# A different instruction order for a chunked attention and wave-MLP kernel on one core

## Chip, cores, metric

One core of one Trainium2 chip. The metric is device time in microseconds (us) of one execution. Times quoted as "profile" times count from the start of the profiled execution's span; the span is some 1.8 us shorter than the timed execution.

## The reference

q, k and v have the shape 8 x 8 heads x 576 x 64. Attention runs within chunks of 64 rows; its output x (8 x 576 x 512) goes through a phase mixing:

```
scores = (q_c @ k_c.T) / 8                  # in chunks of 64 rows
attn   = softmax(scores);  x = attn @ v_c   # x: 8 x 576 x 512
theta  = x @ w_theta                        # 512 x 512
y      = w_tok_r @ (x * cos(theta)) + w_tok_i @ (x * sin(theta))   # 576 x 576
u      = x + y
out    = u + max(u @ w_ch, 0)               # 512 x 512
```

## The kernel before

The work is cut into 327 items. A string, ORDER, lists them; the kernel emits them in that order, so each engine has its own share of the items in that order. Two batches make a pair p (0 to 3), and a pair's rows are cut into five groups g, taken as two 128-row tiles, or one for the middle group, g = 2. An item reads `kind.p.g:bits`:

- `lq`, `lv`: load q and k, or v, of a group; `lw`, `lc`, `lt`: load w_theta, w_ch, w_tok. POOL issues these.
- `a1`: transpose q and k on PE into PSUM, copy both halves out. `a2`: scores on PE, exp on ACT. `a3.p.g.h`: attention times v on PE, reciprocal and product on DVE, giving x.
- `a4`: transpose x (on PE and copied, or by DMA). `a5`: theta on PE, cos and sin on ACT. `z`: x times cos or sin on DVE.
- `tw`: transpose w_tok on PE. `yh` (a half of the columns, only for the first batch) and `y`: the token matmuls and the sum with x. `w`, `ut`, `st`: u @ w_ch, u transposed by DMA, the rest and the store.

The bits say which engine copies: for `a1`, bit 1 puts q's copy on ACT (else DVE), bit 2 puts k's on DVE (else ACT), bit 32 cuts the transposes to 64 x 64 pieces. The parts that the argument touches (cuts marked with `# ...`):

```python
psum = ctx.enter_context(tc.tile_pool(name="psum", bufs=4, space=bass.MemoryType.PSUM))

def psum2(name, dtype=FP32):          # four buffers of 4 KB per partition, in turn
    n = 1024 if dtype == FP32 else 2048
    return psum.tile([P, n], dtype, name=name, tag="ps")

def load_w(ap, f16):
    nc.gpsimd.dma_start(f16, ap.rearrange("(a p) e -> p a e", p=P))

def copy(eng, out, in_):
    if eng: nc.vector.tensor_copy(out=out, in_=in_)
    else:   nc.scalar.copy(out=out, in_=in_)

def a1(p, g, bits):
    ps = psum2("ps_qkT", FP16)
    # ... transposes of q (w = 0) and k (w = 1)
    copy(not bits & 1, qT[...], psv[:, 0, :, :, 0:n])
    copy(bits & 2,     kT[...], psv[:, 1, :, :, 0:n])

def a5(p, g):
    ps = psum2("ps_theta")
    # ... 4 matmuls of 512 columns per 128-row tile, 8 for a group of two tiles
    nc.scalar.activation(out=cos, in_=pin, func=AF.Sin, bias=pihalf, scale=1.0)
    nc.scalar.activation(out=sin, in_=pin, func=AF.Sin)

for n, item in enumerate(ORDER):
    name, bits = item.split(":")
    kind, *args = name.split(".")
    # ...
    emit[kind](*args)
```

The softmax here doesn't subtract the row's maximum and nothing guards it: scores larger than these inputs give would overflow.

Of the kernel before, what the change touches and what calls it, by code (L numbers as in the profile page):

```python
# [16 lines left out]


ORDER = """
lq.0.0:0 lq.0.2:0 lq.0.1:0 a1.0.0:35 lv.0.2:0 lv.0.0:0 lv.0.1:0 lw.0:0 a1.0.2:1 lq.0.3:0  # L20
a2.0.0:0 a2.0.2:0 lq.0.4:0 lt.0.1:0 a1.0.1:2 a3.0.2.0:0 a2.0.1:0 a3.0.0.0:0 a3.0.0.1:0
a3.0.1.0:0 a4.0.2:0 tw.0.0:1 a3.0.1.1:0 lt.1.1:0 lv.0.4:0 a4.0.0:33 a5.0.2:0 a4.0.1:33
z.0.2.0:0 lv.0.3:0 a5.0.0:0 a1.0.3:2 z.0.0.0:0 a5.0.1:0 a1.0.4:3 z.0.1.0:0 z.0.1.1:0
tw.0.2:0 tw.0.1:1 lt.1.0:0 a2.0.4:0 z.0.0.1:0 tw.1.1:0 a2.0.3:0 yh.0.0:0 a3.0.4.0:0
a3.0.4.1:0 yh.0.1:0 tw.1.2:0 a4.0.4:1 a3.0.3.0:0 a3.0.3.1:0 tw.1.0:1 a5.0.4:0 a4.0.3:1
yh.1.0:0 lq.1.0:0 z.0.4.0:0 a1.1.0:0 lq.1.2:0 lq.1.1:0 a1.1.2:1 lq.1.3:0 lc.0:0
z.0.4.1:0 a5.0.3:0 a1.1.1:2 lv.1.2:0 a2.1.0:0 yh.1.1:0 z.0.3.0:0 lv.1.0:0 z.0.3.1:0
a2.1.1:0 lq.1.4:0 a1.1.3:3 lv.1.1:0 lv.1.3:0 a2.1.2:0 lq.2.0:0 w.0.0:0 st.0.0:0
y.0.1.0:0 a3.1.2.0:0 a3.1.0.0:0 lq.2.2:0 lv.1.4:0 lv.2.1:0 w.0.1:0 st.0.1:0 a3.1.0.1:0
w.0.2:0 lq.2.1:0 st.0.2:0 y.0.1.1:0 a4.1.2:32 lv.2.2:0 a3.1.1.0:0 a1.1.4:0 a3.1.1.1:0  # L30
w.0.3:0 st.0.3:0 y.0.1.2:0 lq.2.3:0 a2.1.4:0 a2.1.3:0 a4.1.0:1 a4.1.1:1 a5.1.2:0
a3.1.3.0:0 a1.2.0:2 lv.3.1:0 a5.1.1:0 a3.1.4.0:0 a3.1.4.1:0 lv.2.0:0 y.0.1.3:0 a4.1.4:33
a1.2.2:1 a3.1.3.1:0 w.0.4:0 a5.1.0:0 st.0.4:0 lv.2.3:0 z.1.2.0:0 a1.2.1:3 a4.1.3:33
lq.2.4:0 w.0.5:0 a5.1.4:0 z.1.0.0:0 z.1.1.0:0 z.1.0.1:0 w.0.6:0 st.0.5:0 z.1.1.1:0
st.0.6:2 a5.1.3:0 z.1.3.0:0 lq.3.0:0 y.1.0.0:0 lv.3.4:0 a2.2.2:0 a1.2.3:32 a2.2.1:0
z.1.3.1:0 z.1.4.0:0 z.1.4.1:0 lq.3.2:0 y.1.0.1:0 lv.3.3:0 lq.3.1:0 w.0.7:0 a2.2.0:0
st.0.7:0 a2.2.3:0 y.1.1.0:0 a3.2.2.0:0 a3.2.1.0:0 y.1.1.1:0 a3.2.0.0:0 a3.2.1.1:0
y.1.0.2:0 a4.2.2:0 a3.2.0.1:0 lq.3.3:0 lv.3.2:0 a1.2.4:32 w.0.8:0 st.0.8:0 a5.2.2:0
y.1.0.3:0 a4.2.0:1 a4.2.1:0 a1.3.0:0 a3.2.3.0:0 a1.3.2:1 w.1.0:0 a5.2.0:0 z.2.2.0:0
a5.2.1:0 st.1.0:0 z.2.1.0:0 a3.2.3.1:0 a2.2.4:0 lv.3.0:0 y.1.1.2:0 z.2.0.0:0 lv.2.4:0  # L40
z.2.0.1:0 w.1.1:0 st.1.1:0 y.1.1.3:0 z.2.1.1:0 a2.3.2:0 a2.3.0:0 a1.3.1:35 a3.3.2.0:0
w.1.2:0 lq.3.4:0 st.1.2:0 y.2.0.0:0 a3.3.0.0:0 a3.2.4.0:0 ut.1.1.3:0 y.2.0.1:0 a2.3.1:0
ut.1.1.2:0 a1.3.3:32 a4.2.3:17 a3.2.4.1:0 a4.2.4:16 y.2.0.2:0 a3.3.1.0:0 a2.3.3:0
a1.3.4:35 y.2.0.3:0 ut.1.1.1:0 a2.3.4:0 a3.3.0.1:0 w.1.3:0 st.1.3:2 a3.3.1.1:0
ut.1.1.0:0 w.1.4:0 a4.3.0:49 st.1.4:2 a5.2.3:0 a4.3.1:17 w.1.5:0 a5.2.4:0 a5.3.0:0
st.1.5:2 z.2.4.0:0 z.2.4.1:0 w.1.6:0 a5.3.1:0 w.1.7:0 ut.2.0.1:0 ut.2.0.0:0 z.2.3.0:0
z.2.3.1:0 st.1.6:2 ut.2.0.3:0 st.1.7:2 y.2.1.0:0 a3.3.3.0:0 ut.2.0.2:0 a3.3.4.0:0
y.2.1.1:0 a3.3.4.1:0 a4.3.2:16 a3.3.3.1:0 y.2.1.2:0 a5.3.2:0 w.1.8:0 a4.3.4:16 z.3.0.0:0
z.3.1.0:0 a4.3.3:16 z.3.2.0:0 st.1.8:0 ut.2.1.1:0 z.3.0.1:0 y.2.1.3:0 z.3.1.1:0 w.2.0:0
st.2.0:0 ut.2.1.2:0 a5.3.4:0 w.2.1:0 z.3.4.0:0 z.3.4.1:0 a5.3.3:0 ut.2.1.3:0 st.2.1:0  # L50
w.2.2:0 y.3.0.0:0 st.2.2:2 z.3.3.0:0 z.3.3.1:0 w.2.3:0 ut.2.1.0:0 y.3.0.1:0 w.2.4:0
st.2.3:0 y.3.0.2:0 w.2.5:0 ut.3.0.1:0 st.2.4:0 st.2.5:2 y.3.1.0:0 w.2.6:0 y.3.0.3:0
ut.3.0.2:0 st.2.6:2 ut.3.0.0:0 w.2.7:0 st.2.7:2 y.3.1.1:0 w.2.8:0 st.2.8:2 y.3.1.2:0
ut.3.0.3:0 ut.3.1.1:0 y.3.1.3:0 ut.3.1.0:0 w.3.0:0 st.3.0:2 w.3.1:0 w.3.2:0 ut.3.1.2:0
st.3.1:2 w.3.3:0 ut.3.1.3:0 st.3.2:0 w.3.4:0 st.3.3:0 st.3.4:0 w.3.5:0 w.3.6:0 st.3.5:2
st.3.6:2 w.3.7:0 w.3.8:0 st.3.7:0 st.3.8:0
""".split()


# [572 lines left out]
```

## Time and profile before

| | kernel before |
|---|---|
| timed runs | 209.69, 210.24, 213.06 us |
| profiled execution | 210.18 us, span 208.3 us, mean granted clock 0.971 |
| PE busy | 186.0 us of the span |

The busy table, the slices, the stretches and the waits are in the prediction below. These are lines of PE's timeline; the columns are start, length, engine, source line, operation, output and inputs, sizes, number of instructions, and in brackets the idle time before them and what ended it.

```profile
12.62 1.92 PE L295 MATMUL ps_qkT<-id,qk 128*64 128x128 f16 x32
...
21.83 1.89 PE L443 MATMUL ps_theta<-wtheta,xTm 128*128 128x512 f16 x4 [0.58 <-DMA wtheta<-in_moe_w_theta_dram]
24.38 2.37 PE L443 MATMUL ps_theta<-wtheta,xT 128*128 128x512 f16 x8
...
33.95 0.45 PE L325 MATMUL ps_sT<-qT,kT 64*64 64x64 f16 x32 [2.67 <-DVE kT L212]
...
35.47 1.79 PE L500 MATMUL ps_y<-wT,z 128*128 128x256 f16 x8
...
37.27 1.91 PE L500 MATMUL ps_y<-wT,z 128*128 128x256 f16 x8
...
58.96 2.12 PE L521 MATMUL ps_y<-wT,z 128*128 128x288 f16 x16
...
195.89 7.93 PE L552 MATMUL ps_uw<-wch,uT 128*128 128x512 f16 x36
```

The 32 transposes at 12.62 are item a1.0.1, the two theta groups a5.0.2 and a5.0.0, the 32 small matmuls at 33.95 item a2.0.4, and L500 is yh.0.0, the first real token matmul. Four theta matmuls take as long as eight should (1.89 us): the clock is halved there. yh.0.0's eight (and the eight of its second half at 37.27) take 1.79 and 1.91 us for the same reason, 1.5 us after the wait of 2.67 us. The line at 58.96 is item y.0.1.0, the one at 195.89 PE's last group.

### The profile page before, as it was taken

How to read it: one execution, taken by the hardware profiler on the slowest of the kernel's cores; microseconds unless marked ns; L12 is line 12 of the kernel's file. 1: busy time of each engine (PE TensorE's matmuls, PEld its weight loads, DVE VectorE, ACT ScalarE, POOL GpSimd, SP SyncE). 2: the span in 40 equal slices, each digit the busy share in tenths (PEclk: the TensorE clock that was granted, in tenths of full speed). 3: DMA queues.
4: the chain of work that ended last, by engine and by line, in shares of the span. 5: the costliest groups of instructions: out<-in, count | busy, mean ns of one | idle time of the engine just before them, and what ended most of it. 6: DMA issues, size and time to landing. Idle time of an engine off the chain costs nothing.

```text
span 208.3 us, 7055 instructions
## 1 busy us (share of the span) xinstructions
PE 186.0 (89%) x3150; PEld 124.4 (60%) x3150; DVE 131.2 (63%) x227; ACT 102.3 (49%) x110; POOL 93.5 (45%) x133
## 2 busy tenths in 40 slices
PE   0376894999999999999998999998999999999991
...
PEclk9997599799999999999999999999999999999998
...
GB/s 151 154 159 154 170 200 149 176 184 177 168 147 208 191 198 131 181 27 148 194 138 164 157 146 54 71 81 105 191 166 156 72 142 192 127 130 151 145 264 221
DMA packets 102141, 31.96 MB, mean 153 GB/s; under 512 B 95776, under 2 KB 98208, under 8 KB 102112
## 3 DMA queue, kind: packets, MB, share of 16 engines
...
HBM read 33.06 MB, written 9.44 MB: 204 GB/s over the span
## 4 chain that ended last, share of the span: by engine, by line
PE 70%; ACT 10%; DMA 6%; DVE 5%; issue 4%; POOL 3%; ACTq 0%; POOLq 0%
PE ps_y L521 27%; PE ps_uw L552 14%; PE ps_theta L443 13%; PE ps_y L500 4%; DMA wtheta<-in_moe_w_theta_dram 3%; PE ps_qkT L295 3%; DMA qk<-in_k_dram 3%; PE ps_x L354 3%; DVE kT L212 3%; POOL qk L169 2%; ACT eT L333 2%; PE ps_sT L325 2%; ACT qT L214 2%; ACT cos L453 2%; ACT sin L457 2%
## 5 line engine op out<-in xcount | busy, mean ns | idle before, releaser
L521 PE MATMUL ps_y<-wT,z 128*128 128x288 f16 x448 | 59.6, 286 | 0.3 <-DVE o L575 0.3
L521 PEld LDWEIGHTS <-z 128*128 128x128 f16 x448 | 42.8, 98 | 13.6 <-issue 0.3
L190 POOL DMA_DIRECT2D v<-in_v_dram x56 | 41.8, 773 | 16.1 <-DMA qk<-in_q_dram 6.8
...
L552 PE MATMUL ps_uw<-wch,uT 128*128 128x512 f16 x144 | 37.9, 380 | 0.1
L529 DVE TENSOR_TENSOR uT<-ps_y,xT 128x576 f16<-128x576 f32 x28 | 21.1, 755 | 19.0 <-PE ps_y L521 18.6
L443 PE MATMUL ps_theta<-wtheta,xT 128*128 128x512 f16 x128 | 30.6, 384 | 0.0
L453 ACT ACTIVATE cos<-ps_theta,pihalf 128x1024 f16<-128x1024 f32 (+1 forms) x20 | 20.6, 1031 | 19.6 <-PE ps_theta L443 18.1
L333 ACT ACTIVATE eT<-ps_sT 128x1024 f16<-128x1024 f32 (+1 forms) x20 | 23.1, 1197 | 13.0 <-PE ps_sT L325 12.9
L295 PE MATMUL ps_qkT<-id,qk 64*64 64x64 f16 (+1 forms) x832 | 20.1, 213 | 9.6 <-DMA qk<-in_q_dram 6.8
L368 DVE TENSOR_TENSOR x<-ps_x,recip 128x512 f16<-128x512 f32 x36 | 24.9, 691 | 1.2
L295 PEld LDWEIGHTS <-qk 64*64 64x64 f16 (+1 forms) x832 | 17.3, 114 | 12.4 <-DMA qk<-in_q_dram 6.5
L552 PEld LDWEIGHTS <-uT 128*128 128x128 f16 x144 | 14.0, 98 | 14.4
L212 DVE COPY kT<-ps_qkT 128x1024 f16<-128x1024 f16 x10 | 13.0, 1295 | 13.7 <-ACT qT L214 13.7
L169 POOL DMA_DIRECT2D qk<-in_q_dram x24 | 19.8, 830 | 2.5 <-PE ps_x L354 1.1
L443 PEld LDWEIGHTS <-xT 128*128 128x128 f16 x128 | 11.9, 99 | 14.5 <-DMA xT<-x 0.8
L169 POOL DMA_DIRECT2D qk<-in_k_dram x24 | 19.2, 805 | 1.2 <-issue 0.6
L457 ACT ACTIVATE sin<-ps_theta 128x1024 f16<-128x1024 f32 (+1 forms) x20 | 18.7, 936 | 0.0
L577 DVE SCALAR_TENSOR_TENSOR o<-ps_uw,un 128x512 f32<-128x512 f32 x23 | 15.7, 688 | 2.7 <-PE ps_uw L552 2.2
L468 DVE TENSOR_TENSOR z<-x,cos 128x1024 f16<-128x1024 f16 x16 | 10.8, 686 | 6.1 <-ACT cos L453 6.0
L214 ACT COPY kT<-ps_qkT 128x1024 f16<-128x1024 f16 (+1 forms) x10 | 10.8, 1084 | 6.3 <-DVE qT L212 6.3
L325 PE MATMUL ps_sT<-qT,kT 64*64 64x64 f16 x576 | 8.0, 198 | 5.9 <-DVE kT L212 5.6
...
## 6 DMA issues: line engine op xcount, KB each, us to landing
...
```

Of the source, the lines that this page charges most:

```text
L169: nc.gpsimd.dma_start(t[(pp // 2) : (pp // 2) + m // 2, ti].rearrange("p h t d -> p h (t d)"), src.rearrange("h (p t) d -> p h (t d)", t=2),)
L190: nc.gpsimd.dma_start(v16[pp : pp + m, sl, :, 0:D], v[2 * p + bb, :, s0 : s0 + m, :].rearrange("h s d -> s h d"),)
L212: nc.vector.tensor_copy(out=out, in_=in_)
L295: nc.tensor.transpose(psv[par * D : par * D + D, w, e, tk, r0 // CH : (r0 + step) // CH, :], t[rs, w, 2 * e + par, tk, :], id16[rs, rs],)
L333: nc.scalar.activation(out=eT.rearrange("p (r b s t) -> p r b t s", r=2, s=CH // 2, t=2), in_=ps.rearrange("p r (b t s) -> p r b t s", s=C ...
L368: nc.vector.tensor_tensor(out=xo, in0=px[:, :, :, 0:D], in1=recip.broadcast_to((P, 2, NE, D)), op=ALU.mult,)
L443: nc.tensor.matmul(ps[:, jj * DM : jj * DM + DM], xt[:, db, :], wtheta16[:, db, :], start=(db == 0), stop=(db == NDB - 1),)
L453: nc.scalar.activation(out=cos[:, 0:n].rearrange("p a e -> p (a e)"), in_=pin, func=AF.Sin, bias=pihalf, scale=1.0,)
L457: nc.scalar.activation(out=sin[:, 0:n].rearrange("p a e -> p (a e)"), in_=pin, func=AF.Sin)
L521: nc.tensor.matmul(psv[:, hf, 0:HS], zt[:, db * P : db * P + P], wT[:, kt, hf * HS : hf * HS + HS], start=(kt == 0), stop=(kt == 2 * KT),)
L529: nc.vector.tensor_tensor(out=uT_tile(p)[:, db, sl].rearrange("p (f c) -> p f c", f=2), in0=psv[:, :, 0:HS], in1=xT_tile(p)[:, db, sl].rea ...
L552: nc.tensor.matmul(ps[:, 0:DM], uT[:, db, j * P : j * P + P], wch16[:, db, :], start=(db == 0), stop=(db == NDB - 1),)
```

## The change

The intent: an order found by a search over a model with measured copy and exp times, that issues the first loads later, and that also has to do well in a second scenario where loads and copies take longer. Only the string changes; both strings hold the same 327 items, with other copy bits here and there. The start of the diff (the rest, all of the other items, is replaced in the same way and cut here):

```diff
 ORDER = """
-lq.0.0:0 lq.0.2:0 lq.0.1:0 a1.0.0:35 lv.0.2:0 lv.0.0:0 lv.0.1:0 lw.0:0 a1.0.2:1 lq.0.3:0
-a2.0.0:0 a2.0.2:0 lq.0.4:0 lt.0.1:0 a1.0.1:2 a3.0.2.0:0 a2.0.1:0 a3.0.0.0:0 a3.0.0.1:0
-a3.0.1.0:0 a4.0.2:0 tw.0.0:1 a3.0.1.1:0 lt.1.1:0 lv.0.4:0 a4.0.0:33 a5.0.2:0 a4.0.1:33
-z.0.2.0:0 lv.0.3:0 a5.0.0:0 a1.0.3:2 z.0.0.0:0 a5.0.1:0 a1.0.4:3 z.0.1.0:0 z.0.1.1:0
-tw.0.2:0 tw.0.1:1 lt.1.0:0 a2.0.4:0 z.0.0.1:0 tw.1.1:0 a2.0.3:0 yh.0.0:0 a3.0.4.0:0
+lq.0.0:0 lq.0.2:0 a1.0.0:35 a1.0.2:3 lq.0.1:0 a2.0.0:0 lv.0.2:0 a2.0.2:0 lv.0.0:0
+a1.0.1:1 a3.0.2.0:0 a3.0.0.0:0 lw.0:0 lv.0.1:0 a3.0.0.1:0 a4.0.2:1 lq.0.3:0 a2.0.1:0
+a4.0.0:33 a5.0.2:0 a3.0.1.0:0 a3.0.1.1:0 z.0.2.0:0 a5.0.0:0 lt.0.1:0 a4.0.1:33 a1.0.3:3
+z.0.0.0:0 tw.0.0:1 lq.0.4:0 lt.1.0:0 tw.0.2:1 a5.0.1:0 lv.0.3:0 lt.1.1:0 z.0.0.1:0
+lv.0.4:0 lq.1.0:0 z.0.1.0:0 z.0.1.1:0 lq.1.2:0 tw.0.1:1 a1.0.4:2 lq.1.1:0 a2.0.3:0
+lv.1.2:0 tw.1.0:0 yh.0.0:0 a2.0.4:0 a3.0.3.0:0 lc.0:0 lv.1.0:0 a3.0.3.1:0 lq.1.3:0
 ... (the other lines of both orders cut)
```

More of the change, by code (lines that the diff above doesn't have):

```diff
@@ L19 @@
 ORDER = """
-lq.0.0:0 lq.0.2:0 lq.0.1:0 a1.0.0:35 lv.0.2:0 lv.0.0:0 lv.0.1:0 lw.0:0 a1.0.2:1 lq.0.3:0
-a2.0.0:0 a2.0.2:0 lq.0.4:0 lt.0.1:0 a1.0.1:2 a3.0.2.0:0 a2.0.1:0 a3.0.0.0:0 a3.0.0.1:0
-a3.0.1.0:0 a4.0.2:0 tw.0.0:1 a3.0.1.1:0 lt.1.1:0 lv.0.4:0 a4.0.0:33 a5.0.2:0 a4.0.1:33
-z.0.2.0:0 lv.0.3:0 a5.0.0:0 a1.0.3:2 z.0.0.0:0 a5.0.1:0 a1.0.4:3 z.0.1.0:0 z.0.1.1:0
-tw.0.2:0 tw.0.1:1 lt.1.0:0 a2.0.4:0 z.0.0.1:0 tw.1.1:0 a2.0.3:0 yh.0.0:0 a3.0.4.0:0
-a3.0.4.1:0 yh.0.1:0 tw.1.2:0 a4.0.4:1 a3.0.3.0:0 a3.0.3.1:0 tw.1.0:1 a5.0.4:0 a4.0.3:1
@@ L26 @@
-yh.1.0:0 lq.1.0:0 z.0.4.0:0 a1.1.0:0 lq.1.2:0 lq.1.1:0 a1.1.2:1 lq.1.3:0 lc.0:0
-z.0.4.1:0 a5.0.3:0 a1.1.1:2 lv.1.2:0 a2.1.0:0 yh.1.1:0 z.0.3.0:0 lv.1.0:0 z.0.3.1:0
-a2.1.1:0 lq.1.4:0 a1.1.3:3 lv.1.1:0 lv.1.3:0 a2.1.2:0 lq.2.0:0 w.0.0:0 st.0.0:0
-y.0.1.0:0 a3.1.2.0:0 a3.1.0.0:0 lq.2.2:0 lv.1.4:0 lv.2.1:0 w.0.1:0 st.0.1:0 a3.1.0.1:0
-w.0.2:0 lq.2.1:0 st.0.2:0 y.0.1.1:0 a4.1.2:32 lv.2.2:0 a3.1.1.0:0 a1.1.4:0 a3.1.1.1:0
-w.0.3:0 st.0.3:0 y.0.1.2:0 lq.2.3:0 a2.1.4:0 a2.1.3:0 a4.1.0:1 a4.1.1:1 a5.1.2:0
@@ L32 @@
-a3.1.3.0:0 a1.2.0:2 lv.3.1:0 a5.1.1:0 a3.1.4.0:0 a3.1.4.1:0 lv.2.0:0 y.0.1.3:0 a4.1.4:33
-a1.2.2:1 a3.1.3.1:0 w.0.4:0 a5.1.0:0 st.0.4:0 lv.2.3:0 z.1.2.0:0 a1.2.1:3 a4.1.3:33
-lq.2.4:0 w.0.5:0 a5.1.4:0 z.1.0.0:0 z.1.1.0:0 z.1.0.1:0 w.0.6:0 st.0.5:0 z.1.1.1:0
-st.0.6:2 a5.1.3:0 z.1.3.0:0 lq.3.0:0 y.1.0.0:0 lv.3.4:0 a2.2.2:0 a1.2.3:32 a2.2.1:0
-z.1.3.1:0 z.1.4.0:0 z.1.4.1:0 lq.3.2:0 y.1.0.1:0 lv.3.3:0 lq.3.1:0 w.0.7:0 a2.2.0:0
-st.0.7:0 a2.2.3:0 y.1.1.0:0 a3.2.2.0:0 a3.2.1.0:0 y.1.1.1:0 a3.2.0.0:0 a3.2.1.1:0
@@ L38 @@
-y.1.0.2:0 a4.2.2:0 a3.2.0.1:0 lq.3.3:0 lv.3.2:0 a1.2.4:32 w.0.8:0 st.0.8:0 a5.2.2:0
-y.1.0.3:0 a4.2.0:1 a4.2.1:0 a1.3.0:0 a3.2.3.0:0 a1.3.2:1 w.1.0:0 a5.2.0:0 z.2.2.0:0
-a5.2.1:0 st.1.0:0 z.2.1.0:0 a3.2.3.1:0 a2.2.4:0 lv.3.0:0 y.1.1.2:0 z.2.0.0:0 lv.2.4:0
-z.2.0.1:0 w.1.1:0 st.1.1:0 y.1.1.3:0 z.2.1.1:0 a2.3.2:0 a2.3.0:0 a1.3.1:35 a3.3.2.0:0
-w.1.2:0 lq.3.4:0 st.1.2:0 y.2.0.0:0 a3.3.0.0:0 a3.2.4.0:0 ut.1.1.3:0 y.2.0.1:0 a2.3.1:0
-ut.1.1.2:0 a1.3.3:32 a4.2.3:17 a3.2.4.1:0 a4.2.4:16 y.2.0.2:0 a3.3.1.0:0 a2.3.3:0
@@ L44 @@
-a1.3.4:35 y.2.0.3:0 ut.1.1.1:0 a2.3.4:0 a3.3.0.1:0 w.1.3:0 st.1.3:2 a3.3.1.1:0
-ut.1.1.0:0 w.1.4:0 a4.3.0:49 st.1.4:2 a5.2.3:0 a4.3.1:17 w.1.5:0 a5.2.4:0 a5.3.0:0
-st.1.5:2 z.2.4.0:0 z.2.4.1:0 w.1.6:0 a5.3.1:0 w.1.7:0 ut.2.0.1:0 ut.2.0.0:0 z.2.3.0:0
-z.2.3.1:0 st.1.6:2 ut.2.0.3:0 st.1.7:2 y.2.1.0:0 a3.3.3.0:0 ut.2.0.2:0 a3.3.4.0:0
-y.2.1.1:0 a3.3.4.1:0 a4.3.2:16 a3.3.3.1:0 y.2.1.2:0 a5.3.2:0 w.1.8:0 a4.3.4:16 z.3.0.0:0
-z.3.1.0:0 a4.3.3:16 z.3.2.0:0 st.1.8:0 ut.2.1.1:0 z.3.0.1:0 y.2.1.3:0 z.3.1.1:0 w.2.0:0
@@ L50 @@
-st.2.0:0 ut.2.1.2:0 a5.3.4:0 w.2.1:0 z.3.4.0:0 z.3.4.1:0 a5.3.3:0 ut.2.1.3:0 st.2.1:0
-w.2.2:0 y.3.0.0:0 st.2.2:2 z.3.3.0:0 z.3.3.1:0 w.2.3:0 ut.2.1.0:0 y.3.0.1:0 w.2.4:0
-st.2.3:0 y.3.0.2:0 w.2.5:0 ut.3.0.1:0 st.2.4:0 st.2.5:2 y.3.1.0:0 w.2.6:0 y.3.0.3:0
-ut.3.0.2:0 st.2.6:2 ut.3.0.0:0 w.2.7:0 st.2.7:2 y.3.1.1:0 w.2.8:0 st.2.8:2 y.3.1.2:0
-ut.3.0.3:0 ut.3.1.1:0 y.3.1.3:0 ut.3.1.0:0 w.3.0:0 st.3.0:2 w.3.1:0 w.3.2:0 ut.3.1.2:0
-st.3.1:2 w.3.3:0 ut.3.1.3:0 st.3.2:0 w.3.4:0 st.3.3:0 st.3.4:0 w.3.5:0 w.3.6:0 st.3.5:2
@@ L56 @@
-st.3.6:2 w.3.7:0 w.3.8:0 st.3.7:0 st.3.8:0
+lq.0.0:0 lq.0.2:0 a1.0.0:35 a1.0.2:3 lq.0.1:0 a2.0.0:0 lv.0.2:0 a2.0.2:0 lv.0.0:0
[4 more added lines that the diff above has]
+lv.1.2:0 tw.1.0:0 yh.0.0:0 a2.0.4:0 a3.0.3.0:0 lc.0:0 lv.1.0:0 a3.0.3.1:0 lq.1.3:0
```

31 lines of the change are left out of this document (added).

## The prediction

> **What bounds the kernel now.** I read the page's busy table first, then its slices, then the busy time by stretch, then PE's waits, then the timeline of the first 56 us.
>
> ```profile
> PE 186.0 (89%) x3150; PEld 124.4 (60%) x3150; DVE 131.2 (63%) x227; ACT 102.3 (49%) x110; POOL 93.5 (45%) x133
> ...
> PE   0376894999999999999998999998999999999991
> PEclk9997599799999999999999999999999999999998
> ```
>
> PE is the bound, and from the eighth slice on (5.2 us each) it is full. So an order that keeps PE's work can only win in the first seven slices, in the small holes later, and in the slices whose granted clock is low (7, 5 and 7 tenths in the fourth, fifth and eighth). The stretches, cut at the ends of PE's large waits, say how much:
>
> ```profile
> 0.00:6.50 6.50, 0.00 (x0) 0.00 (x0) 0.94 (x3) 1.28 (x1) 5.35 (x13) 1.00 0.90 151
> 6.50:15.00 8.50, 5.85 (x192) 5.07 (x192) 1.71 (x2) 4.13 (x5) 8.01 (x11) 1.00 1.89 159
> 15.00:21.80 6.80, 3.87 (x146) 3.02 (x140) 5.87 (x14) 3.17 (x4) 5.80 (x8) 0.76 1.56 153
> 21.80:31.30 9.50, 9.45 (x128) 5.00 (x128) 5.48 (x10) 5.87 (x7) 4.52 (x6) 0.81 1.62 187
> 31.30:34.00 2.70, 0.05 (x4) 0.05 (x8) 1.40 (x2) 2.68 (x4) 2.02 (x3) 1.00 1.98 133
> 34.00:39.30 5.30, 5.30 (x103) 3.82 (x106) 2.60 (x5) 3.25 (x3) 5.07 (x8) 0.68 1.51 171
> ...
> 50.00:100.00 50.00, 48.94 (x1001) 32.90 (x995) 36.72 (x62) 35.53 (x41) 32.44 (x44) 1.00 1.56 156
> 100.00:150.00 50.00, 47.99 (x1003) 33.53 (x1002) 33.43 (x61) 29.73 (x32) 16.30 (x23) 1.00 1.08 128
> 150.00:204.00 54.00, 53.80 (x402) 33.15 (x400) 34.81 (x58) 12.10 (x14) 6.11 (x12) 1.00 0.67 158
> ```
>
> The columns are the stretch, its length, busy time of PE, PEld, DVE, ACT, POOL, then granted clock, DMA share and GB/s. PE idles 6.5 us for the first q, 2.65 us to 15 us, 2.93 us to 21.8 us, 2.65 us from 31.3 to 34 us, and only 1.06 + 2.01 + 0.20 = 3.3 us from 50 to 204 us. The clock costs (1 - 0.81) x 9.5 = 1.8 us and (1 - 0.68) x 5.3 = 1.7 us of full-speed work. After the last matmul, 4.4 us remain. What PE waits for from 21.8 to 40 us:
>
> ```profile
> PE ps_sT L325 <- DVE kT L212: 2.7, 1, 2.7
> PE ps_theta L443 <- DMA wtheta<-in_moe_w_theta_dram: 0.6, 1, 0.6
> ```
>
> **What the Trainium skill says.** "TensorE: Matmul & The Clock Gate", section "Part 1: The HAM clock gate": the array's clock is halved by default and after an idle window of about 3.4 us, and returns after about as long of sustained work. The trace agrees in kind: low clock follows both idle spells, and a 512-column theta matmul takes 634 ns at worst against a median of 379 ns. "ScalarE: Activation LUTs", "What ACT_TABLE_LOAD costs": about 1283 ns per switch of table plus a drain of 1380 ns. The trace has 1283 ns each time and the next activation 20 ns later, so no drain beside it. "PSUM — Partial Sum Buffer", "PSUM bank collisions raise a hardware error": two engines, two readers too, must be kept off the same bank and quadrant. The trace has the guard: when the q half of an a1 tile is copied by ACT, DVE starts the k half only as ACT ends (10.33 to 10.36 us); the waits of this kind sum to 13.7 us. Splitting the two copies over two engines therefore shortens nothing; it only chooses whose queue is loaded. "DMA: Bandwidth & Descriptors", "Issuing engines are not separate DMA queues": moving a transfer between POOL and SP saves issue time at most. Nothing in this trace contradicts it; outputs land in 2.6 us from POOL and 3.3 us from SP.
>
> **The change part by part.** Both orders hold the same 327 items.
>
> *PE's work.* Six of the large a1 use 64-row pieces in both, only partly the same ones. a4 goes from 56 full and 144 quarter transposes to 60 and 128. At 0.54 us for eight full ones and 0.45 us for 32 quarter ones this is under 0.1 us. Number of DMA transposes is equal. So PE's work is unchanged: 0.
>
> *ACT and DVE.* Of the large copies, q moves 4 from DVE to ACT, xT 5 from DVE to ACT; the four small k copies move from ACT to DVE, three small q too, and two small wT copies go to ACT. ACT pays about 1.01 us for a large copy and 0.6 to 0.75 us for a small one: 9 x 1.01 - 7 x 0.68 + 2 x 0.5 - 0.6 + 0.6 = about +5 us on 102. DVE loses about as much. Table switches: I counted the exp and sin runs in ACT's order, 9 changes in both. None of it is on PE's path by itself.
>
> *The start.* Here the order really changes. A walk with the durations of this trace (my own arithmetic, us from the start):
> - To 14.5 us nothing differs: q lands 6.5, k 8.6, first exp at 12.4, both exps done 14.3.
> - Before, DVE copies both halves of a1.0.1 (14.6 to 16.5), so the first reciprocal waits until 16.4 and the a2.0.1 product is put ahead of a3.0.0 on PE. After, ACT, idle there, does these copies (14.6 to 16.9), DVE does x of a3.0.2 at once, and a3.0.0 starts when its v lands at 17.34 as before.
> - w_theta is issued before lv.0.1 instead of behind it, three issues earlier. In the trace the stretch between v.0.0 landing (17.3) and w_theta landing (21.8) holds both loads; w_theta's part is about half, so it lands near 19.5. x of the middle group is then in xT at about 20.1, which is the later of the two. a5.0.2 starts at 20.1 instead of 21.8: 1.7 us.
> - From there PE runs a3.0.1 (two), a5.0.0, a4.0.1, a1.0.3, tw.0.0, tw.0.2, a5.0.1 (27.9), tw.0.1 (30.0), a1.0.4, a2.0.3, and tw.1.0 once the sines of a5.0.1 have freed its buffer (32.0). yh.0.0 waits for tw.0.1's copy on ACT, at 33.0. Before, yh.0.0 starts at 35.5, after the same work plus a2.0.4 (0.4 us) and with tw.1.1 in place of tw.1.0. Gain 2.5 - 0.4 = **2.1 us**.
> - The wait of 2.7 us at 31.3 has gone, so the clock should not fall again from 34 to 39 us: 1.7 us, taken as **1.5 us**.
> - Going on to the end of yh.1.1, with PSUM's four buffers in turn, gives 50.8 us with a1.1.1 and a2.1.0 (1.01 + 0.38 us) still to do, so 52.2 against 55.9 before: 3.7 us, which agrees with the sum of 3.6 us.
>
> *Loads.* Landing times read from POOL's waits: q.0.3 24.5, k.0.3 25.5, q.0.4 26.9, k.0.4 28.3, first w_tok_i piece 29.8 us. In the new sequence that piece would land near 27.0 (needed 27.2), qk.0.4 near 29.8 (needed 30.5), the second w_tok_i near 31.6 (needed 32), v.0.3 near 33.8 (needed 35.6). All just in time: I put a 30% chance on some 2 us lost, 0.6 us.
>
> *Middle and tail.* The holes from 50 us on are 3.3 us now. Reordering could take half of them or add as much; I count 0. The last items (two y, nine w) are the same, so the last 12 us stay.
>
> Sum: -2.1 - 1.5 + 0.6 = -3.0 us on 210.2: **207.2 us**.
>
> **The rivals.**
> 1. *The loads pace the start.* The DMA share stays near or above 1.5 (two queues are counted) in the first 50 us and POOL waits for landings from 22 us on. If the loads come 2 us later than my walk, PE waits at tw.0.2, a1.0.4 or a3.0.3 in place of a2.0.4, and the clock falls again. For it: margins under 1 us. Against it: PE waited only 0.6 us on a load between 18 and 40 us before. Time then about 209 to 210.
> 2. *The middle improves as well.* The order was found with measured copy and exp times, so it may remove PE's holes at 57, 81, 114, 131 to 143 us. At most 3.3 us more, half likely: 204 to 205.5. Against it: these holes are small and spread, and new ones come with any order.
> 3. *ACT becomes late in the middle.* 5 us more copies on ACT, between 57 and 120 us, where it is about 70% busy and once (110 to 120) 86%. An a4 copy on ACT queues behind sin and exp, and theta waits. It would cost 1 to 3 us: 208.5 to 210.
>
> **Range and chances.** The start's gain has a spread of about 1.5 us, the middle of about 1.5 us, run to run some 0.5 us; together about 2.2 us, so 8 in 10 is 204.2 to 209.8. A gain over 2% needs under 206.0: the start as computed and a part of rival 2, chance 0.28. Slower by over 2% needs two new large stalls, 0.03. The rest, 0.69, is within 2%.
>
> **What would show it right or wrong.** Right: the first theta matmul near 20.1 us, the first yh near 33 us, no PE wait over 1 us between 22 and 40 us, a granted clock over 0.9 from 34 to 39 us, the last L500 group ending near 51 us, PE busy about 182 to 184 us with the same 3150 matmuls. Wrong: a PE wait on a DMA of w_tok_i, qk or v between 26 and 36 us (rival 1); PE idle under 1.5 us from 50 us on (rival 2); PE waits on ACT copies summing over 2 us after 50 us (rival 3). If PE's busy time stays at 186 us though idle fell, the clock step failed.

## The result

| | before | after |
|---|---|---|
| timed runs, us | 209.69, 210.24, 213.06, 216.46 | 203.03, 203.26, 204.05, 204.15 |
| median | 211.65 | 203.66 |
| profiled span | 208.3 | 202.3 |
| mean granted clock there | 0.971 | 1.000 |

The ratio of fast runs is 0.970 (95% interval 0.964 to 0.976): faster. Here and below a ratio is the mean time of one kernel's fast runs over the mean of the other's fast runs of the same rounds, so it is not quite the ratio of the medians; two of the four runs of the kernel before were not fast, and its fast runs were near 210 us. The fast gain is thus some 6.3 us and the spans differ by 6.0 us. The prediction had 3.0 us.

The page of the kernel after, its busy line, PE's slices and the clock:

```profile
PE 183.8 (91%) x3138; PEld 123.9 (61%) x3138; DVE 129.6 (64%) x223; ACT 108.6 (54%) x114; POOL 94.8 (47%) x135
...
PE   0378989999999999999999699999999999999991
...
PEclk9999999999999999999999999999999999999999
```

PE is busy for 2.2 us less, and its slices from the fourth to the seventh read 8, 9, 8, 9 in place of 6, 8, 9, 4; one slice in the middle has dropped to 6. ACT works 6.3 us longer, where about 5 us were counted. The same stretches as in the prediction, of the kernel after:

```profile
6.50:15.00 8.50, 5.37 (x176) 4.57 (x176) 1.91 (x2) 3.50 (x4) 8.07 (x11) 1.00 1.90 161
15.00:21.80 6.80, 5.90 (x156) 3.58 (x155) 4.28 (x11) 5.61 (x6) 6.21 (x9) 1.00 1.73 175
21.80:31.30 9.50, 8.34 (x172) 5.44 (x170) 8.25 (x15) 7.99 (x10) 4.42 (x7) 1.00 1.65 193
31.30:34.00 2.70, 2.68 (x70) 2.24 (x73) 2.03 (x3) 2.03 (x2) 2.49 (x4) 1.00 1.54 155
34.00:39.30 5.30, 5.16 (x120) 4.02 (x107) 4.17 (x9) 2.81 (x3) 4.95 (x8) 1.00 1.74 159
...
50.00:100.00 50.00, 49.31 (x1000) 33.98 (x996) 35.94 (x63) 35.01 (x40) 31.68 (x44) 1.00 1.54 166
...
100.00:150.00 50.00, 48.08 (x975) 32.41 (x964) 35.26 (x62) 32.88 (x33) 17.58 (x25) 1.00 1.11 129
```

From 15 to 21.8 us PE works 5.90 us in place of 3.87 (in part because the same work takes longer there: the clock is halved throughout, as shown below, where the kernel before had it in full from 15.1 to 18.5 us), and from 31.3 to 34 us it works 2.68 us in place of 0.05. From 50 to 150 us its idle time hardly moved: 0.69 + 1.92 us against 1.06 + 2.01.

The granted clock of 1.00 before 21.8 us must not be believed. In every trace the clock records alternate between half and full, so a record stands only where the clock changes. The first one of this execution is at 21.6 us, so the page prints full clock before it without having seen it. The lengths tell what was so; PE's timeline of the kernel after:

```profile
13.17 1.92 PE L295 MATMUL ps_qkT<-id,qk 128*64 128x128 f16 x32
16.16 0.65 PE L354 MATMUL ps_x<-v,eT 64*64 64x65 f16 x31 [0.44 <-DMA v<-in_v_dram]
...
19.10 1.86 PE L443 MATMUL ps_theta<-wtheta,xTm 128*128 128x512 f16 x4
21.48 1.93 PE L443 MATMUL ps_theta<-wtheta,xT 128*128 128x512 f16 x8
...
30.44 0.62 PE L233 MATMUL ps_wT<-id,wnat 128*128 128x128 f16 x8 [0.48 <-DMA wnat<-in_moe_w_tok_r_dram]
...
31.54 1.05 PE L500 MATMUL ps_y<-wT,z 128*128 128x256 f16 x8
...
32.53 1.04 PE L500 MATMUL ps_y<-wT,z 128*128 128x256 f16 x8
...
53.43 2.13 PE L521 MATMUL ps_y<-wT,z 128*128 128x288 f16 x16
...
190.30 7.93 PE L552 MATMUL ps_uw<-wch,uT 128*128 128x512 f16 x36
```

Four theta matmuls at 19.10 take 1.86 us, half clock; eight at 21.48 take 1.93 us, full clock. So the clock was halved up to 21.6 us and full from there to the end of PE's work. In the kernel before the records say: full at 15.1, half at 18.5, full at 25.4, half at 35.6, full at 39.0 us. In every trace two changes lie 3.41 us or a whole multiple of it apart; where these steps fall differs from one execution to the next.

What PE waits for from 22 to 40 us in the kernel after:

```profile
PE ps_wT L233 <- DMA wnat<-in_moe_w_tok_r_dram: 0.7, 2, 0.5
PE ps_wT L233 <- DVE xT L212: 0.3, 1, 0.3
PE ps_qkT L295 <- DMA qk<-in_k_dram: 0.2, 1, 0.2
```

The wait of 2.7 us is gone and nothing large stands in its place.

**Where the 6.0 us come from.** I use three landmarks on PE's timeline: the first yh (item yh.0.0), the first full token matmul (item y.0.1.0), and the start of PE's last group.

| us | before | after | gain of the stretch that ends here |
|---|---|---|---|
| first theta | 21.83 | 19.10 | |
| yh.0.0 | 35.47 | 31.54 | 3.93 |
| y.0.1.0 | 58.96 | 53.43 | 1.60 |
| PE's last group | 195.89 | 190.30 | 0.06 |
| end of the span | 208.3 | 202.3 | 0.4 |

PE does the same items ahead of y.0.1.0 in both kernels, except one of 1.01 us (a1.1.3) replaced by one of 1.09 us (w.0.1). The item a2.0.4, 0.38 us, stands ahead of yh.0.0 before and behind it after. So, for the same work, the gain up to yh.0.0 is 3.93 - 0.38 = 3.55 us, and the one between yh.0.0 and y.0.1.0 is 1.60 + 0.38 + 0.08 = 2.06 us. From y.0.1.0 to the last group the two profiles need 136.93 and 136.87 us, the same. These are one execution each. Kernels below that share a start show the spread: y.0.1.0 comes at 52.72 to 54.41 us in four fast profiles of the new start, at 58.31 and 58.96 us in two of the old one. So the gain of some 5 us is clear of it, and differences of 1 us between single profiles are not.

### The profile page after: what moved, and what is told of

Same layout as the page of the kernel before. It is cut to its first block, busy times and chain, and to the rows that moved or that the text cites. A ratio compares the mean times of both kernels' runs of the same rounds, so it can differ in the third digit from the quotient of the medians.

```text
span 202.3 us, 7032 instructions
## 1 busy us (share of the span) xinstructions
PE 183.8 (91%) x3138; PEld 123.9 (61%) x3138; DVE 129.6 (64%) x223; ACT 108.6 (54%) x114; POOL 94.8 (47%) x135
## 4 chain that ended last, share of the span: by engine, by line
PE 73%; DMA 12%; DVE 5%; ACT 4%; POOL 2%; issue 2%; ACTq 0%; POOLq 0%
PE ps_y L521 30%; PE ps_uw L552 15%; PE ps_theta L443 11%; DMA wnat<-in_moe_w_tok_r_dram 5%; PE ps_y L500 4%; PE ps_qkT L295 4%; DMA qk<-in_k_dram 3%; DMA wtheta<-in_moe_w_theta_dram 3%; PE ps_sT L325 2%; PE ps_x L354 2%; PE ps_xT L417 2%; DVE kT L212 2%; POOL v L190 1%; ACT qT L214 1%; ACT xT L214 1%
## 5 line engine op out<-in xcount | busy, mean ns | idle before, releaser
L587 POOL DMA_DIRECT2D out_dram<-o x18 | 9.9, 553 | 83.6 <-DVE o L577 49.4
L295 PEld LDWEIGHTS <-qk 64*64 64x64 f16 (+1 forms) x832 | 17.3, 115 | 11.0 <-DMA qk<-in_q_dram 7.6
L212 DVE COPY kT<-ps_qkT 128x1024 f16<-128x1024 f16 (+1 forms) x14 | 15.8, 1135 | 11.7 <-ACT qT L214 11.7
L577 DVE SCALAR_TENSOR_TENSOR o<-ps_uw,un 128x512 f32<-128x512 f32 x23 | 15.8, 689 | 5.4 <-PE ps_uw L552 3.8
L214 ACT COPY qT<-ps_qkT 128x1024 f16<-128x1024 f16 (+1 forms) x11 | 10.7, 976 | 11.7 <-PE ps_qkT L295 11.6
L575 DVE TENSOR_TENSOR o<-ps_uw,o 128x512 f32<-128x512 f32 x13 | 9.0, 689 | 7.0 <-ACT o L568 7.0
```

The costliest lines, as they stand in the source:

```text
L295: nc.tensor.transpose(psv[par * D : par * D + D, w, e, tk, r0 // CH : (r0 + step) // CH, :], t[rs, w, 2 * e + par, tk, :], id16[rs, rs],)
```

## The experiments

All ratios are against the kernel before, run in the same rounds. Where the profiled execution of a run fell in the slow state it is said, and then only lengths at full clock or differences within it are read.

| run | ratio (95%) | first theta | yh.0.0 | y.0.1.0 | from there to last group |
|---|---|---|---|---|---|
| new start, old rest | 0.973 (0.964 to 0.983) | 18.91 | 31.41 | 54.41 | 136.7 |
| old start, new rest | 0.988 (0.978 to 0.999) | 22.02 s | 37.59 s | 62.59 s | 135.1 s |
| filler in the wait | 0.994 (0.987 to 1.001) | 22.67 s | 36.29 s | 58.11 s | 141.3 s |
| new, more early work | 0.980 (0.964 to 0.995) | 18.77 s | 33.34 s | 55.33 s | 143.6 s |
| new, w_theta late | 0.977 (0.967 to 0.986) | 21.43 | 33.51 | 55.51 | 137.2 |
| old, w_theta early | 1.009 (1.003 to 1.016) | 23.07 | 36.33 | 59.65 | 139.2 |
| old, new first copies | 1.013 (1.006 to 1.020) | 20.37 | 36.83 | 59.09 | 140.3 |
| old, both of these | 1.000 (0.991 to 1.008) | 18.63 | 35.61 | 57.91 | 136.6 |
| old, new middle of the start | 0.994 (0.984 to 1.003) | 21.44 | 32.70 | 56.41 | 138.5 |
| new, theta behind y | 0.977 (0.968 to 0.985) | 18.89 | 30.73 | 52.72 | 139.1 |
| old, theta later | 1.001 (0.994 to 1.009) | 21.98 | 35.75 | 58.31 | 139.1 |
| new, whole transposes | 0.972 (0.967 to 0.976) | 19.44 | 31.86 | 53.85 | 137.1 |

(s: the profiled execution was slow.)

### Which half of the order

The two orders were cut at y.0.1.0 and crossed: the items up to it from one order, the remaining ones as the other order has them.

```diff
# s_after_r_before                        # s_before_r_after
- <old order up to y.0.1.0>               + <old order up to y.0.1.0>
+ <new order up to y.0.1.0>               - <old order's remaining items>
  <old order's remaining items>           + <new order's remaining items>
```

> The new order up to (not including) y.0.1.0, then the old order for whatever is left. Both orders have done almost the same PE work there (w.0.1 of 1.09 us in place of a1.1.3 of 1.01 us), and the two traces reach y.0.1.0 at 53.4 and 59.0 us, so theory 'the start is all of the gain' expects 203.5 to 204.8 us, ratio to before about 0.97 to 0.975, and a span near 202.7. The rival 'the middle gives a part' expects 206 or more. A seam between two orders can itself cost up to 1 us.

> The old order up to y.0.1.0, then the new one. The start theory expects no gain beyond 0.5 us, about 209.5 to 210.5; the rival that the middle carries half of the gain expects about 207.

Measured: the new start with the old rest has fast runs of 204.15 to 207.04 us, median 205.09 where 203.5 to 204.8 was expected, ratio 0.973. The old start with the new rest has fast runs of 207.30, 207.71 and 210.34 us, ratio 0.988. So the start carries most of it, as the theory had it. The second half was worth more than the 0.5 us that I allowed it, about 1.2%, but with an interval from 0.1% to 2.2%. The last column of the table says why one profile can't narrow this: in six fast profiles that leave the old rest as it is, it took from 136.6 to 140.3 us; in two that leave the new one as it is, 136.9 and 137.2. The new rest seems the steadier one, on few executions. The slow profile of the old start with the new rest points the same way: its clock records show no change from 41.4 to 208.7 us, so the rest ran at full clock there, and took 135.1 us, less than in any other profile.

### The clock after the wait

The claim: the wait of 2.7 us makes the clock fall from 35.5 to 38.9 us. In the old order, PE was given work to do inside that wait, into the buffer that the next item overwrites, so the result stays correct:

```diff
 def a2(p, g):
     ps = psum2("ps_sT")
+    if (p, g) == (0, 4):
+        for _ in range(10):
+            nc.tensor.matmul(ps[:, 0:DM], id16, wtheta16[:, 0, :])
```

> The old order with ten idle-work matmuls (128x512, result overwritten) put into the wait of 2.7 us ahead of the a2.0.4 product. They shorten no wait. Clock theory: PE stays busy, so the clock doesn't fall at 34 us, the first yh matmuls of 256 columns take about 0.11 us in place of 0.21, and the time falls by 1.3 to 1.8 us (208.3 or so). Rival: the low clock at 34 us comes from elsewhere, or what follows is held by loads; then 0 or slightly slower.

PE's timeline of this run (its profiled execution was slow):

```profile
22.67 1.89 PE L446 MATMUL ps_theta<-wtheta,xTm 128*128 128x512 f16 x4 [0.91 <-DMA wtheta<-in_moe_w_theta_dram]
...
32.52 2.32 PE L320 MATMUL ps_sT<-wtheta,id 128*128 128x512 f16 x10 [0.44 <-ACT sin L460]
34.77 0.45 PE L328 MATMUL ps_sT<-qT,kT 64*64 64x64 f16 x32
...
36.29 1.05 PE L503 MATMUL ps_y<-wT,z 128*128 128x256 f16 x8
```

The wait is not shorter: a2.0.4 follows the first theta by 12.10 us, before by 12.12. But yh.0.0's eight matmuls take 1.05 us, not 1.79, and from the first theta to y.0.1.0 it is 35.43 us in place of 37.13. The 1.7 us are gone with the wait still there: the low clock after the wait is what they were. The time, 0.994 (0.987 to 1.001), fits 1.7 us but does not show it alone, and this is one execution.

The other traces say how firm the claim is. Six profiles have this wait of 2.67 us unfilled. In five of them the clock is halved within 1.7 us of its end (in the slow one 0.6 us before its end), for 3.4 us or, in the slow one, 6.8 us. In the sixth, the run with both parts below, it isn't: that run's records show full clock from 26.3 us on. In the eight profiles that lack the wait or have it filled, the clock is not halved between 27.5 and 60 us. So the wait makes the fall likely, not certain. That it depends on how the wait lies in the steps of 3.41 us fits this, but no run here tests it.

If that was so cheap, could the halved clock up to 21.6 us in the new order (21.4 in the expectation, misread by 0.2 us) be removed too? Matmuls on the identity were put where PE idles at the start (28 ahead of the first q, 10 between q and k of a1.0.0, 8 ahead of a2.0.0):

```diff
 # new order
+ warm(28)   # behind make_identity: 28 x nc.tensor.matmul(warm_ps[:, 0:P], id16, id16)
 # a1.0.0, between the q and the k transposes
+ warm(10)
 # a2.0.0, ahead of the scores
+ warm(8)
```

> The new order with 28 idle-work matmuls on the identity while PE waits for the first q, 10 while it waits for the first k and 8 ahead of the first a2. In the new trace the clock is first granted in full at 21.4 us; a1.0.1 took 1.92 us (1.0 at full clock) and the first theta 1.86 (1.24). Clock theory: full clock from about 8 to 11 us on, first theta at most 0.5 us earlier as its loads bind, everything behind it 0.5 to 1.2 us earlier, 202.5 to 203.2 us. Rival: the loads bind until 21 us and nothing is gained, or the clock falls back before 21 us as PE is too idle.

The stretches of this run (profiled in the slow state; the third column from the end is the granted clock):

```profile
6.50:15.00 8.50, 6.50 (x199) 5.30 (x197) 1.92 (x2) 4.31 (x5) 8.50 (x12) 0.80 1.94 168
15.00:21.80 6.80, 5.11 (x152) 2.99 (x152) 3.83 (x10) 5.11 (x6) 6.02 (x8) 0.66 1.77 181
21.80:31.30 9.50, 9.50 (x134) 5.52 (x125) 6.44 (x12) 5.25 (x7) 4.72 (x7) 0.71 1.63 193
```

The full clock was granted early, at 6.9 us, but the records have it halved again at 10.3 and at 17.1 us, the second time until 27.3 us. Where the new order alone has full clock, from 21.8 to 31.3 us, this one has 0.71: with PE busy throughout, (1 - 0.71) x 9.5 = 2.8 us of full-speed work are lost there. Its two fast runs were 205.03 and 207.55 us, slower than the new order where 202.5 to 203.2 us was expected: missed. In the execution profiled, the clock won early was lost again, and the second loss fell where PE is full. That this is why the fast runs were slower is not shown, as none of them was profiled.

### What in the start

Three things that differ in the first 36 us were tried: w_theta's load stands ahead of lv.0.1; the copies and items up to a5.0.2 are placed otherwise; the items between a5.0.1 and yh.0.0 too. (The later loads, and the items between a5.0.2 and a5.0.1, also stand in another order; they were not tried apart.) First w_theta's place alone, in either order:

```diff
# after_lw_back: new order                # b_lw: old order
-a3.0.0.0 lw.0 lv.0.1 a3.0.0.1            -lv.0.0 lv.0.1 lw.0 a1.0.2
+a3.0.0.0 lv.0.1 lw.0 a3.0.0.1            +lv.0.0 lw.0 lv.0.1 a1.0.2
```

> The new order with the one load of w_theta moved back behind lv.0.1. If the earlier w_theta is what makes the start faster, the first theta matmul goes from 19.1 back to 21 to 21.8 us and the time rises by 1.5 to 2.5 us (205.5 to 206). If w_theta was not binding and the freed DVE and the order of PE are the cause, it rises by under 0.7 us.

> The old order with w_theta issued ahead of lv.0.1 and nothing else. In the old trace PE comes to the first theta only at 21.25 us, 0.6 us before the load lands, so my theory that load and copies must move together expects the first theta at 21.2 us or so, and 0.3 to 0.7 us off the time (ratio 0.997). The rival 'the load is the cause, the rest is decoration' expects 2 us off (ratio 0.99).

PE's timeline of the first, then of the second:

```profile
21.43 1.86 PE L442 MATMUL ps_theta<-wtheta,xTm 128*128 128x512 f16 x4 [1.97 <-DMA wtheta<-in_moe_w_theta_dram]
```

```profile
19.51 0.23 PE L353 MATMUL ps_x<-v,eT 64*64 64x65 f16 x1 [1.50 <-DMA v<-in_v_dram]
20.52 0.43 PE L353 MATMUL ps_x<-v,eT 64*64 64x65 f16 x15 [0.78 <-DMA v<-in_v_dram]
23.07 1.89 PE L442 MATMUL ps_theta<-wtheta,xTm 128*128 128x512 f16 x4
```

In the new order it is worth what its theory said: with w_theta behind lv.0.1, PE waits 1.97 us for it, the first theta comes at 21.43 in place of 19.10, and y.0.1.0 2.1 us later. In the old order the same move makes it worse, by 0.9%, where 0.3 to 0.7 us off was expected: the item a3.0.1 stands ahead of the first theta on PE, and its v, now behind w_theta in the queue, comes late (waits of 1.50 and 0.78 us). The early load is only worth something together with PE's order, which puts a3.0.1 behind the first theta.

So next the copies and places of the first items in the old order, without and with the load's move:

```diff
# b_copies (b_both: the same and lw.0 ahead of lv.0.1), old order
-a1.0.2:1 ... a1.0.1:2 a3.0.2.0 a2.0.1 a3.0.0.0 a3.0.0.1 a3.0.1.0 a4.0.2:0 tw.0.0 a3.0.1.1 ... a4.0.0 a5.0.2 a4.0.1
+a1.0.2:3 ... a1.0.1:1 a3.0.2.0 a3.0.0.0 a3.0.0.1 a4.0.2:1 a2.0.1 a4.0.0 a5.0.2 a3.0.1.0 tw.0.0 a3.0.1.1 ... a4.0.1
```

> The old order with the copies of a1.0.1 on ACT, a3.0.0, a4.0.2, a2.0.1, a4.0.0 and the first theta in the new sequence, but w_theta still behind lv.0.1. The joint theory expects PE to wait for w_theta for about 2 us, the first theta at 21.5 to 22.5 us, and no gain (ratio 0.995 to 1.005). The rival 'freeing DVE is the cause' expects 1.5 to 2 us off.

> Both edits together. The joint theory expects the first theta near 19 us, and about 2.0 to 2.7 us off the time (ratio 0.987 to 0.99), with the second wait ahead of the first yh still there or moved earlier. If the gains were additive and small, about 0.5 us off.

PE's timeline of the run with both:

```profile
18.63 1.89 PE L442 MATMUL ps_theta<-wtheta,xTm 128*128 128x512 f16 x4
23.26 0.53 PE L416 MATMUL ps_xT<-id,x 64*64 64x64 f16 x24 [0.93 <-DVE x L367]
23.73 3.17 PE L442 MATMUL ps_theta<-wtheta,xT 128*128 128x512 f16 x8
...
34.09 0.45 PE L324 MATMUL ps_sT<-qT,kT 64*64 64x64 f16 x32 [2.67 <-DVE kT L211]
...
35.61 1.06 PE L499 MATMUL ps_y<-wT,z 128*128 128x256 f16 x8
```

The first theta comes as early as in the new order, 18.63 us, so these two parts together do what the prediction's walk said they do. But the gain does not stay. a4.0.1 stands between the first theta and a5.0.0, as it did before, and now waits 0.93 us for x; a5.0.0 starts at 23.73 us (21.48 in the new order), mostly at half clock, which this execution had until 26.3 us; and the wait of 2.67 us before a2.0.4 is there as ever. yh.0.0 begins at 35.61, where it did before, y.0.1.0 is 1.05 us earlier, and the time is the same (1.000). The 1.05 us are no gain of these parts: in this execution the clock did not fall after the wait (yh.0.0 takes 1.06 us, before 1.79), which alone is worth 1.6 us there. I had expected 2.0 to 2.7 us off: missed. With the copies alone it is 1.3% slower, where no change was expected; the first theta at 20.37 us was earlier than I had expected, again without anything left of it at yh.0.0 (36.83).

Last, the items between a5.0.1 and yh.0.0 nearly as the new order has them (without its loads, and with tw.1.1 for tw.1.0), in the old order:

```diff
# b_second, old order
-a5.0.1 a1.0.4:3 z.0.1.0 z.0.1.1 tw.0.2 tw.0.1 lt.1.0 a2.0.4 z.0.0.1 tw.1.1 a2.0.3 yh.0.0 a3.0.4.0
+a5.0.1 lt.1.0 z.0.0.1 z.0.1.0 z.0.1.1 tw.0.2 tw.0.1 a1.0.4:2 a2.0.3 tw.1.1 yh.0.0 a2.0.4 a3.0.4.0
```

> The old order, changed only from a5.0.1 to yh.0.0: z of the second group and both w_tok copies ahead of a1.0.4, which DVE copies whole, a2.0.3 ahead and a2.0.4 behind yh.0.0, as in the new order. The wait of 2.7 us at 31.3 should shrink to under 1 us and the clock should stay up at 34 us: 2 to 3.5 us off (ratio 0.984 to 0.99). The rival, that the loads pace this stretch, expects a DMA wait (tw.1.1 or qk) in its place and under 1 us off.

PE's timeline of it:

```profile
32.70 1.05 PE L499 MATMUL ps_y<-wT,z 128*128 128x256 f16 x8
...
36.62 0.45 PE L353 MATMUL ps_x<-v,eT 64*64 64x65 f16 x32 [1.41 <-ACT eT L332]
...
140.65 1.26 PE L520 MATMUL ps_y<-wT,z 128*128 128x288 f16 x9 [1.78 <-issue]
```

This does what was expected of it at the landmarks: the wait of 2.7 us has gone, yh.0.0 runs at full clock, and y.0.1.0 comes 2.55 us earlier, although a wait of 1.41 us on an exp has appeared behind yh.0.0. Yet the time moves by 0.6% only (0.984 to 1.003): from y.0.1.0 on the profile is 1.6 us longer than before, and one hole of 1.78 us at 140.65 us, marked "issue", is enough for that.

So of the 5.53 us by which y.0.1.0 is earlier in the new order, the third part alone makes 2.55 us, some of it the clock after the wait, and the two first parts nothing once the clock is set aside. Some 3 us did not come from any part alone (single profiles, with the spread named above). All three parts together in the old order were not run. What the timelines suggest, then, is not shown: an early first theta is of use where a5.0.0 follows it at once, and the wait behind a5.0.1 is gone.

### The hole in the middle

One slice of the kernel after fell to 6 tenths. PE's and ACT's timeline there:

```profile
112.93 1.89 PE L443 MATMUL ps_theta<-wtheta,xT 128*128 128x512 f16 x8
113.21 1.02 ACT L457 ACTIVATE sin<-ps_theta 128x1024 f16<-128x1024 f32 x1
...
116.32 2.13 PE L521 MATMUL ps_y<-wT,z 128*128 128x288 f16 x16 [1.50 <-ACT cos L453]
```

The label blames a cosine on ACT, which looks like my rival 3. But y.1.1.2 (at 116.32) needs the PSUM buffer of the theta whose sine is the ACT line shown, and that ended at 114.23 us; PE was free at 114.82. The cosine named is only the last event that the profile saw before the start. A rival: PE had no instructions. The page's part 3 has a queue for them:

```profile
q8 instruction: 24, 0.39, 0.8%
```

Its columns are fetches, MB and share: 24 fetches, 0.39 MB, so 16 KB each. In the trace one of them starts at 113.86 us, and PE resumes at 116.32, 2.45 us later. The first matmul of y.1.1.2 is row 4270 of PE's list of instructions (weight loads and matmuls counted). Two theories, two kernels. If the buffer (or ACT) is the cause, moving that theta behind y.1.1.2 takes the wait away; if the supply is, the hole stays near the same place of the list:

```diff
# after_swap: new order                      # after_pieces: new order
-a5.2.0 z.2.1.0 y.1.1.2                      -a1.3.0:35
+z.2.1.0 y.1.1.2 a5.2.0                      +a1.3.0:3
```

> The new order with the theta group a5.2.0 moved behind y.1.1.2, where the new trace has PE's largest later hole, 1.5 us put down to ACT's cosine. The program makes y.1.1.2 wait only for the sine of a5.2.1 there, done 2.1 us before the matmul started. If ACT's copies and sines are late (my rival 3), the swap gives them a y's 2.2 us more and the hole goes: about 1 to 1.5 us off the new order. If PE's own supply of instructions is the cause (a burst of some 200 small ones comes just before, and the record calls part of the hole 'issue'), a hole of 1 to 1.5 us stays at about 113 to 115 us whatever is next in the queue, and the time is that of the new order.

PE's timeline of after_swap:

```profile
112.05 1.14 PE L520 MATMUL ps_y<-wT,z 128*128 128x288 f16 x8
115.59 1.15 PE L520 MATMUL ps_y<-wT,z 128*128 128x288 f16 x8 [2.40 <-issue]
```

The hole has moved into the middle of y.1.1.2, between its eighth and ninth matmul: the buffer is already in use there, and the tiles of z and w_tok that are read had been read by y.1.1.1 before. The ninth is again row 4270, and PE resumes 2.46 us after the start of a fetch at 113.13. So late instructions explain it, and ACT is cleared of this hole. The same pattern stands behind the other holes of this kind: in nine kernels with 13 of them, 0.53 to 2.40 us long, PE resumes at a row whose remainder by 256 (what one fetch holds, to judge by 24 fetches for some 6280 rows) is between 168 and 182, 2.3 to 3.0 us after a fetch began (the kernel after: row 4270, remainder 174; old, new middle of the start: row 5288, remainder 168, 2.39 us; old, theta later: row 5290, remainder 170, 2.98 us). Kernel after_swap is 2 us slower than the new order; its trace has the hole 0.9 us longer and two new waits behind it, 0.66 us on a sine and 0.65 us on a copy.

Can it be avoided? The transposes of a1.3.0, cut to 64-row pieces by its bit 32, run ahead of the hole, where 256 rows pass in 5.3 us. Without the bit (half as many transposes of double the rows) the list is used up more slowly:

> The new order with a1.3.0 in 32 transposes of 128 rows in place of 64 of 64 rows: 0.46 us more PE work, 64 fewer PE instructions. In five traces PE stood still for 0.65 to 2.4 us, and in each it resumed 2.3 to 2.9 us after the start of one of the 24 fetches of PE instructions (16 KB each), at rows of PE's list that are 168 to 182 modulo 256; in the new order that is row 4270, the first matmul of y.1.1.2, whatever stands there. With this edit row 4270 falls into a2.3.2, behind a whole y, so PE takes 8.2 us in place of 5.3 for the 256 rows before it and the fetch should be in time. Supply theory: no hole over 0.6 us from 100 to 125 us, 0.5 to 1.1 us off the new order, 202.5 to 203.2 us, ratio 0.963 to 0.968. Rival (ACT's cosine): the hole stays at y.1.1.2, and the time is 0.4 us over the new order's.

The stretch from 100 to 125 us, of the kernel after and of after_pieces:

```profile
100.00:125.00 25.00, 23.43 (x504) 16.62 (x493) 18.34 (x34) 17.13 (x18) 14.26 (x19) 1.00 1.53 135
```

```profile
100.00:125.00 25.00, 25.00 (x491) 17.93 (x490) 19.22 (x36) 17.04 (x18) 14.78 (x20) 1.00 1.57 141
```

PE's timeline of after_pieces, later:

```profile
134.28 0.29 PE L353 MATMUL ps_x<-v,eT 64*64 64x65 f16 x12 [1.03 <-issue]
```

The hole is gone and PE is busy in all of that stretch, but new ones of 1.03 and 0.53 us appear at 134.28 and 138.56 us. The time, with six fast runs from 203.86 to 204.75 us, has the ratio 0.972, beside 0.970 for the new order: no better. So no run here beat the new order. Why one fetch is late and most are not stays open.

One more possible reason for the second half: the old order lets theta's weight loads wait for a DMA transpose of x between 131 and 146 us (0.8 us in all in the kernel before, 1.5 us in the new start with the old rest). That theta was moved behind:

```diff
# b_theta_late: old order
-w.1.6 a5.3.1 w.1.7 ... a5.3.2 w.1.8
+w.1.6 w.1.7 ... a5.3.2 a5.3.1 w.1.8
```

> The old order with the one theta group a5.3.1 moved later, ahead of w.1.8. In the old order PE reaches it as its transposed x, sent over DMA, lands: no slack in the first trace, waits of 1.2 to 2.6 us in the traces of three variants with the old second half, none in those with the new. If that is part of what the second half is worth, no theta waits on a DMA of x any more and the time is 0.5 to 1.5 us lower (ratio 0.993 to 0.998). If the waits only showed in variants, no change.

No theta waits on a transpose any more, but a hole of 1.92 us marked "issue" at 142.54 us is there instead, and the ratio is 1.001. That wait is thus not shown to be what the second half is worth.

## Why the prediction was right or wrong

By its own steps:

- **The direction and the places were right.** Its marks came out: the first theta was to come near 20.1 us and came at 19.10, yh.0.0 near 33 us and came at 31.54, PE's largest wait between 22 and 40 us is 0.5 us, the clock from 34 to 39.3 us is 1.00, PE is busy for 183.8 us (182 to 184 predicted). The last L500 group ends at 49.2 us where 51 was given. Cutting and crossing the orders confirms that the start carries most of the gain.
- **The most likely class was wrong, and the result lies at the edge of the range.** The median of 203.66 us is 0.5 us below the lower end of 204.2; the ratio of fast runs, taken on the 210.2 us that the prediction started from, gives 203.9 us (202.6 to 205.1). "Within 2%" had 0.69. What failed is the size of terms, not the mechanism. The terms were 2.1 + 1.5 - 0.6 = 3.0 us; measured in the profiles are 3.55 + 2.06 - 0 = 5.6 us, of 6.0 in all. The other 0.4 us are in the tail behind PE's last group, which I had at 0.
- **The start, 2.1 us, was 3.55.** Two errors of the walk show in the timeline. It lets a3.0.0 wait for its v until 17.34 us as before; v landed early enough for it to run at 16.16 (and q had landed 0.7 us later than before, 7.21 against 6.53), so the first theta was 1.0 us earlier than walked. This goes with the load's own move: the last piece of v.0.0 lands at 15.8 to 16.2 us in six profiles in which w_theta follows it in the queue, and at 16.4 to 17.3 us in seven in which lv.0.1 does. And a5.0.0 follows at 21.48 us already at full clock, eight matmuls in 1.93 us, where before they took 2.37. That is partly luck: in the other three fast profiles of the same start full clock came at 22.3, 23.7 and 24.1 us.
- **The clock, 1.5 us, was 2.06**, this with small holes in it. The clock's own part: yh.0.0 and the second half of it took 1.79 + 1.91 us in place of 1.05 + 1.04, that is 1.6 us of it. The filler run shows the cause, in one execution: the wait kept, the low clock gone, 1.7 us earlier at y.0.1.0. The prediction takes the fall as bound to the wait; it came in five of six profiles.
- **The loads, 0.6 us of risk, cost nothing that I could find.** w_tok_r comes 0.7 us late in two waits and k 0.2 us, inside a gain that is larger all the same. Rival 1 is out.
- **The middle, 0, is right in the two first profiles** (136.93 and 136.87 us) **and unsettled in the timed runs**: the new rest on the old start gains 1.2% with an interval of 0.1 to 2.2%. Rival 2, under 1.5 us of PE idle from 50 us on, is wrong: 2.6 us against 3.3. Rival 3's mark, waits on ACT's copies over 2 us, did not come; the one wait named after ACT was late instructions.
- **Slips:** "the same 3150 matmuls" contradicts the prediction's own count of 4 more full and 16 fewer quarter transposes, which gives 3138, as the page has it. The 13.7 us of waits on ACT's q copies are all of DVE's idle time before six k copies and not only what the guard cost: ahead of the first, 5.21 us of them, the transposes of k ended just 0.2 us before the copy. An activation that waits for nothing else starts 11 or 12 ns after a table load, not 20.

What the prediction doesn't say is how far the parts need each other. It walks the new order as a whole, so its sum did not depend on that; but it books 2.1 us to the start and 1.5 us to the vanished wait side by side. Alone, w_theta's early load costs 0.9% and the copies 1.3% in the old order, both together give nothing, and the third part gives 2.55 us at y.0.1.0.

Open: what the second half is worth between 0 and 2%, whether the three parts of the start suffice together, what decides whether the clock falls after the wait, and what makes single instruction fetches late.

## What to carry to other kernels

Order changes need not be sums: here an earlier load paid only where the engine's own order let the first user run, and an earlier first user, it seems, only where the next big item follows it. A wait that is followed by a halved clock costs more than its length, and the same wait may or may not be followed by one in a given execution; look at the lengths of the same instruction behind it, and do not trust a granted clock printed ahead of the first record. When a hole's releaser had long been done, or the hole lies inside one accumulation, look at the instruction fetches before blaming an engine.

## What the Trainium skill lacked or had wrong

- "Runtime: NRT & Kernel Launch", section "Instruction fetch mechanics": it says that crossing a 16 KiB block of 256 instructions is "mostly hidden". The fetches of 16 KB agree (24 of them, 0.39 MB). But PE stood still for 0.53 to 2.40 us at such places, resuming 2.3 to 3.0 us after a fetch began; the page gives no sign by which to tell such a hole, nor its size.
- "TensorE: Matmul & The Clock Gate", section "Part 1: The HAM clock gate": about 3.4 us of sustained work release the clock. The section does not say how dense the work has to be: in the kernel after, PE was busy for 5.37 of 8.5 and 5.90 of 6.8 us, and the full clock came only at 21.6 us; with 46 filler matmuls it came at 6.9 us and fell twice again, with PE busy for 6.50 of 8.5, 5.11 of 6.8 and 9.50 of 9.5 us and a mean granted clock of 0.80, 0.66 and 0.71 in these stretches. And the idle window of about 3.4 us that it names for the fall was not needed whole: an idle time of 2.67 us was followed by a halved clock in five of six profiles.
- No page that I read says that what PE waits for can be mislabelled by the profile where the instructions were late: "<-ACT cos" for 1.50 us in the kernel after, "<-issue" for 2.40 us at the same row of the list in after_swap.
